# Where the row sums of a pair of heads are finished in a fused attention and expert kernel

## The chip, the cores and the metric

The kernel runs on one core of one Trainium2 chip. The metric is the device time of one execution in microseconds (us); less is better. The engines are TensorE (PE; its weight loads are listed apart as PEld), VectorE (DVE), ScalarE (ACT), GpSimd (POOL) and SyncE (SP, which issues most DMAs). Each engine carries out its own instructions in the order in which the built program holds them and waits at semaphores for the others.

## The reference

Two stages follow each other. The first is causal attention over 8 batches, 8 heads, 576 positions and 64 columns, with a bias from a running sum; the second sends each of the 4608 rows to one of 8 experts.

```python
scores = scale * q @ k.T                       # 576 x 576 for each batch and head
cum = np.cumsum(np.maximum(s, 0.0), axis=-1)
bias = -(cum[:, :, :, None] - cum[:, :, None, :])
scores = np.where(causal, -1000000000.0, scores + np.minimum(bias, 0.0))
attn = np.exp(scores - scores.max(-1))
attn = attn / (np.sum(attn, axis=-1, keepdims=True) + 1e-09)
x = attn @ v                                   # then 4608 x 512
...
h = np.maximum(x[mask] @ w1[e], 0.0)           # for each expert e
out[mask] = gate_w[mask, None] * (h @ w2[e])
```

The division by the row sum plus 1e-9 is the step that is moved here.

## The kernel before, in words

Attention works on 32 pairs. A pair is the same head of two batches, a and b. It is cut into nine chunks: chunk i below 8 holds 128 queries, of batch a for 0 to 3 and b for 4 to 7, against the 128, 256, 384 or 512 keys that the mask leaves; chunk 8, the joint chunk, holds the last 64 queries of both against all 576 keys. The chunks come in the order 3, 7, 2, 6, 8, 1, 5, 0, 4.

For each chunk PE makes the scores in a PSUM tile `sp`, a first product at L376 and a second at L398 (L416 and L417 for the joint chunk, twice two of each). DVE adds the mask and takes the row maximum in one instruction (L400, L422), with a short second one that reads out the maximum. ACT takes the exponent (L431) and leaves the row sum in one column of `sums`; the reading of that sum shows as a second short instruction on ACT.

Three chunks later (`LAG`) PE transposes the exponents into a PSUM tile `pt` (L451; L466 for the joint chunk), of which there are two, used in turn. ACT copies `pt` to `PT` in SBUF (L455); for the joint chunk DVE does (L469, L471). A transpose that wants a `pt` tile therefore waits until the copy from two tiles before is done. Chunks 1 and 5 share one tile and one copy, and so do 0 and 4.

The generator `whole` finishes a pair while the next pair's scores run. One step after the last transposes it makes the value products of PE (L538: into `o` for the first 512 queries of each head, into a tile of the `sp` kind for the last 64), copies `o` by ACT and the other by DVE into `oT`, and yields. At its next step, one chunk later in the text, it takes the row sums: ACT adds `eps`, which holds 1e-9, to the nine columns of `sums` and writes `rs`; DVE takes the reciprocal in place. Then PE multiplies `oT` by a matrix that also holds the router's weights (L350, into `xo`, named `ox` in the profile), and DVE multiplies the result by `rs` into `x` (L560, L562). The second half of the rows (g = 1) goes first, the first half six chunks later (`XLAG`).

What stands where in an engine's queue is decided by a scheduler in the framework, which starts from the order of the code. `issue_after` binds an instruction behind another: the row sums come behind the newest row maximum (`hold`) and the newest exponent (`act`).

Beside this, POOL splits q and k into high and low parts (L326, L330), and the router's steps for a group of eight pairs run in small pieces on DVE, ACT and PE. The experts follow, with matmuls at L1225 and L1199.

Of the kernel before, what the change touches and what calls it, by code (L numbers as in the profile page):

```python
# [7 lines left out]
F32 = mybir.dt.float32  # L8
# [3 lines left out]
AF = mybir.ActivationFunctionType  # L12
# [5 lines left out]
P = 128  # L18
# [24 lines left out]
class Attn:  # L43
# [475 lines left out]
    def whole(self, st):  # L519

        nc = self.nc
        V, PT, x, h = st["V"], st["PT"], st["x"], st["h"]
        for _ in range(TD):
            yield
        o, ox = st["o"], self.ps1.tile([P, 512], F32, name="sp", bufs=SPB)
        oT = self.oT

        pe, self.pe = self.pe, []
        for j in range(5):
            for q0, q1, t, b in ((P * j, 512, o, 0), (512, KW, ox, 512)):  # L530
                if q0 == q1:
                    continue
                for ab in range(2):
                    r = slice(64 * ab, 64 * ab + 64)
                    with ExitStack() as after:
                        for i in pe:
                            after.enter_context(self.tc.issue_after(i))
                        m = nc.tensor.matmul(t[r, q0 - b:q1 - b], V[:, ab, j, :], PT[:, ab, PTS * j + q0 if j < 4 else PTW - 64:PTS * j + q1 if j < 4 else PTW], start=j == 0, stop=j == (4 if b else 3))  # L538
                pe = [m.ins]
        self.wall = m.ins  # L540
        nc.scalar.copy(oT[:, :512], o)
        for ab in range(2):
            r = slice(64 * ab, 64 * ab + 64)
            nc.vector.tensor_copy(oT[r, 512 + 64 * ab:576 + 64 * ab], ox[r, :64])
        yield
        rs = self.sm.tile([P, 9], F32, name="rs")
        with self.tc.issue_after(self.hold[0]), self.tc.issue_after(self.act):
            nc.scalar.activation(rs, st["sums"], AF.Identity, bias=self.eps[:, :1])  # L548
            nc.vector.reciprocal(rs, rs)
        xo = self.xo  # L550
        for g in (1, 0):
            for u in range(2):
                c = 2 * g + u
                with self.tc.issue_after(self.pe[-1]):
                    self.pw_(xo[:, 2 * XW * u:2 * XW * u + 2 * XW], oT[:, P * c:P * c + P], self.pw[:, h, :], start=True, stop=True)
            if g:
                self.pw_(xo[:, 4 * XW:5 * XW], oT[:, 512:], self.pq[:, h, :], start=True, stop=True)
            src = xo[:, :4 * XW].rearrange("p (t d) -> p t d", t=4)
            rv = rs[:, 4 * g:4 * g + 4].unsqueeze(2).broadcast_to([P, 4, XW])
            nc.vector.tensor_tensor(x[g][:, :, :, h], src.rearrange("p t (d r) -> p t d r", r=2), rv.rearrange("p t (d r) -> p t d r", r=2), ALU.mult)  # L560
            if g:
                nc.vector.tensor_scalar(x[2][:, 0, :, h], xo[:, 4 * XW:5 * XW].rearrange("p (d r) -> p d r", r=2), rs[:, 8:9], None, ALU.mult)  # L562
                for _ in range(XLAG if st["pi"] % 8 < 7 and st["pi"] < 30 else 1):
                    yield
# [999 lines left out]
```

## Time and profile before

| what | value |
|---|---|
| median of 3 runs | 785.98 us (785.61 to 785.99) |
| the profiled execution | 786.53 us |
| its span, first to last instruction | 784.8 us |
| PE busy | 772.5 us (98% of the span) |
| PEld busy | 667.4 us (85%) |
| DVE busy | 544.5 us (69%) |
| ACT busy | 501.0 us (64%) |
| POOL busy | 366.3 us (47%) |
| granted TensorE clock, mean | 0.996 |

The profile is of one execution. In its rows, a time in square brackets is how long the engine stood idle before the instruction, and behind the arrow is what ended that. A row of the waits gives the total in us, how often, and the longest. In a timeline the columns are start, duration, engine, line, operation, tiles and shapes, and a count where equal instructions that follow each other are merged. Matmuls overlap, and their ends are modelled, so a row of PE tells when a matmul starts better than when it ends.

### The profile page before, as it was taken

How to read it: one execution, taken by the hardware profiler on the slowest of the kernel's cores; microseconds unless marked ns; L12 is line 12 of the kernel's file. 1: busy time of each engine (PE TensorE's matmuls, PEld its weight loads, DVE VectorE, ACT ScalarE, POOL GpSimd, SP SyncE). 2: the span in 40 equal slices, each digit the busy share in tenths (PEclk: the TensorE clock that was granted, in tenths of full speed). 3: DMA queues.
4: the chain of work that ended last, by engine and by line, in shares of the span. 5: the costliest groups of instructions: out<-in, count | busy, mean ns of one | idle time of the engine just before them, and what ended most of it. 6: DMA issues, size and time to landing. Idle time of an engine off the chain costs nothing. (4 is left out here: it accounts for less than half of the span.)

```text
span 784.8 us, 17146 instructions
## 1 busy us (share of the span) xinstructions
PE 772.5 (98%) x5764; PEld 667.4 (85%) x5764; DVE 544.5 (69%) x1422; ACT 501.0 (64%) x1145; POOL 366.3 (47%) x386
## 2 busy tenths in 40 slices
PE   7999999999999999999999999999999999999997
PEld 6888888888888888888888999998889998998882
DVE  7675577655776667767879797877777877778311
ACT  6877878778787788886565435555555555455211
POOL 8978887898789978994710111110110111110011
PEclk9999999999999999999999999999999999999999
DMA  7477556677567665758979989787788787887760
GB/s 232 133 227 234 189 191 192 212 249 211 163 191 236 211 201 159 248 179 240 324 254 299 325 250 328 249 264 250 238 261 274 250 253 244 271 261 241 256 214 31
DMA packets 88169, 181.21 MB, mean 231 GB/s; under 512 B 13786, under 2 KB 33114, under 8 KB 87951
## 3 DMA queue, kind: packets, MB, share of 16 engines
q1 hardware_dynamic: 82238, 160.03, 65.0%
q0 software_dynamic: 5840, 20.06, 6.6%
q8 instruction: 46, 0.75, 0.4%
q14 instruction: 45, 0.36, 0.1%
HBM read 143.59 MB, written 26.80 MB: 217 GB/s over the span
## 5 line engine op out<-in xcount | busy, mean ns | idle before, releaser
L1211 POOL DMA_INDIRECT out<-ys,oi x36 | 41.1, 1142 | 337.2 <-ACT ys L1210 244.1
L431 ACT ACTIVATE pe<-pe,mx 128x512 f32<-128x512 f32 (+3 forms) x256 | 142.3, 559 | 12.3 <-DVE mx L400 12.2
L400 DVE CUSTOM_DVE_ANT_0 pe<-sp,mk 128x512 f32<-128x512 f32 (+3 forms) x256 | 116.6, 480 | 43.0 <-ACT rs L548 24.0
L455 ACT COPY PT<-pt 128x512 f32<-128x512 f32 (+1 forms) x192 | 94.1, 504 | 26.9 <-PE pt L451 26.9
L451 PE MATMUL pt<-ident,pe 128*128 128x128 f32 x640 | 106.1, 278 | 0.2 <-ACT pe L431 0.2
L376 PE MATMUL sp<-KA,QH 128*128 128x256 f32 (+2 forms) x256 | 98.6, 390 | 1.3 <-POOL KA L240 1.3
L1227 ACT ACTIVATE hT<-hp 128x512 fp32r<-128x512 f32 x72 | 43.1, 599 | 85.9 <-PE hp L1225 85.9
L330 POOL TENSOR_TENSOR QL<-rawq,QH 64x576 fp32r<-64x576 f32 x62 | 87.1, 1422 | 0.3
L330 POOL TENSOR_TENSOR KA<-rawk,KA 64x576 fp32r<-64x576 f32 x62 | 86.4, 1412 | 0.1
L1225 PE MATMUL hp<-xT,wcb 128*128 128x256 f32 x648 | 86.0, 277 | 0.0
L398 PE MATMUL sp<-KB,QL 76*128 76x256 f32 (+2 forms) x256 | 84.1, 330 | 1.7 <-DMA QL<-ek 1.6
L538 PE MATMUL o<-PT,V 128*64 128x512 f32 (+1 forms) x496 | 84.5, 440 | 0.0
L451 PEld LDWEIGHTS pt<-ident,pe 128*128 128x128 f32 x640 | 77.4, 144 | 7.6 <-ACT pe L431 1.4
L1228 DVE SCALAR_TENSOR_TENSOR hT<-hp,hT 128x512 fp32r<-128x512 f32 x72 | 49.5, 688 | 47.1 <-ACT hT L1227 46.7
L1225 PEld LDWEIGHTS hp<-xT,wcb 128*128 128x128 f32 x648 | 79.9, 188 | 0.6
L1199 PE MATMUL y<-wcb,hT 128*128 128x512 f32 x336 | 79.5, 393 | 0.0
L1199 PEld LDWEIGHTS y<-wcb,hT 128*128 128x128 f32 x336 | 62.5, 188 | 13.2
L1225 PE MATMUL hp<-xT,wca 128*128 128x256 f32 x528 | 72.3, 277 | 0.0
L1225 PEld LDWEIGHTS hp<-xT,wca 128*128 128x128 f32 x528 | 66.0, 188 | 0.7 <-DVE hT L1228 0.2
L538 PEld LDWEIGHTS sp<-PT,V 128*64 128x64 f32 x620 | 38.2, 137 | 33.3 <-issue 28.8
L1225 PE MATMUL hp<-xT,wcc 128*128 128x256 f32 x456 | 63.0, 277 | 1.5 <-DVE hT L1228 1.5
L1199 PE MATMUL y<-wca,hT 128*128 128x512 f32 x264 | 62.3, 392 | 0.0
(294 smaller groups left out, 1633.8 us busy)
## 6 DMA issues: line engine op xcount, KB each, us to landing
wrbw<-in_w SPq DMA_DIRECT2D x94, 512.0 KB
wraw<-in_w SPq DMA_DIRECT2D x50, 512.0 KB
rawq<-in_qkv SPq DMA_DIRECT2D x31, 576.0 KB
rawk<-in_qkv SPq DMA_DIRECT2D x31, 576.0 KB
V<-in_qkv SPq DMA_DIRECT2D x32, 320.0 KB
KB<-KA SPq DMA_DIRECT2D x62, 144.0 KB
xr<-lists SPq DMA_DIRECT2D x68, 128.0 KB
wcb<-in_w SPq DMA_DIRECT2D x10, 512.0 KB
```

Of the source, the lines that this page charges most:

```text
L330: self.last = nc.gpsimd.tensor_tensor(o, i, h, ALU.subtract).ins
L376: self.pe.append(self.nc.tensor.matmul(sp[:, :nn], QH[:, q0:q0 + P], self.KA[u][:, ab, :nn], start=True, stop=False).ins)
L398: self.pe.append(nc.tensor.matmul(sp[:, :nn], QL[:EXT, q0:q0 + P], KB[:EXT, ab, :nn], start=False, stop=True).ins)
L400: ins = nc.vector.tensor_tensor_reduce(out=t[:, :n], in0=sp[:, :n], in1=self.mk[:, 512 - n:512], scale=-0.125, scalar=3.0e38, op0=ALU.add, ...
L431: self.act = nc.scalar.activation(t[:, :n], t[:, :n], AF.Exp, bias=m, scale=-1.0, accum_out=st["sums"][:, o:o + 1]).ins
L451: self.pe.append(nc.tensor.transpose(out=pt[:, o:o + P], in_=pe[:, P * j:P * j + P], identity=self.ident).ins)
L455: return cp(w[:, :, :, v:v + P], pt[:, :n * (1 + both)].rearrange("p (a j q) -> p a j q", a=1 + both, q=P))
L538: m = nc.tensor.matmul(t[r, q0 - b:q1 - b], V[:, ab, j, :], PT[:, ab, PTS * j + q0 if j < 4 else PTW - 64:PTS * j + q1 if j < 4 else PTW], ...
L1199: self.last[0] = nc.tensor.matmul(y[u], hT[:, a, f, P * u:P * u + P], W[4 + f // 2][:, c, 512 * (f % 2):512 * (f % 2) + 512], start=f == 0 ...
L1225: nc.tensor.matmul(hp[:, u], W[k][:, a, f:f + P], xT[:, c, k], start=k == 0 and i == 0, stop=k == 3 and i == 2)
L1227: hi = nc.scalar.activation(hs, hp, AF.Relu)
L1228: lo = nc.vector.scalar_tensor_tensor(hT[:, 1, 2 * m:2 * m + 2], hp, 0.0, hs.bitcast(F32), ALU.max, ALU.subtract)
```

## The change

Four lines of `whole` move up: the row sums and their reciprocal are written into the program ahead of the copies of the value products instead of behind the yield that follows them. The same instructions are issued with the same shapes.

```diff
         self.wall = m.ins
+        rs = self.sm.tile([P, 9], F32, name="rs")
+        with self.tc.issue_after(self.hold[0]), self.tc.issue_after(self.act):
+            nc.scalar.activation(rs, st["sums"], AF.Identity, bias=self.eps[:, :1])
+            nc.vector.reciprocal(rs, rs)
         nc.scalar.copy(oT[:, :512], o)
         for ab in range(2):
             r = slice(64 * ab, 64 * ab + 64)
             nc.vector.tensor_copy(oT[r, 512 + 64 * ab:576 + 64 * ab], ox[r, :64])
         yield
-        rs = self.sm.tile([P, 9], F32, name="rs")
-        with self.tc.issue_after(self.hold[0]), self.tc.issue_after(self.act):
-            nc.scalar.activation(rs, st["sums"], AF.Identity, bias=self.eps[:, :1])
-            nc.vector.reciprocal(rs, rs)
         xo = self.xo
```

In the changed kernel the row sums are line 543, the reciprocal 544, the ACT copy 545 and the DVE copies 548. The scheduler gives another order than the text alone would tell. On ACT, at the end of a pair (here the twenty-first; the `pe` tile is that of the next pair's chunk 1, numbered 3807 before and 3810 in the change):

```order
-L541 COPY oT<-o 128x512
-L455 COPY PT_110<-pt 128x4x128
-L431 ACTIVATE pe_3807,sums<-pe_3807,mx 128x256
-L548 ACTIVATE rs<-sums,eps 128x9
+L543 ACTIVATE rs<-sums,eps 128x9
+L545 COPY oT<-o 128x512
+L455 COPY PT_110<-pt 128x4x128
+L431 ACTIVATE pe_3810,sums<-pe_3810,mx 128x256
 L455 COPY PT_110<-pt 128x3x128 x2
```

The row sums stood between the exponent of chunk 1 and the two copies of chunks 2 and 6; now they stand ahead of the copy of the value products, and those two copies follow the exponent. A few rows further on ACT (`pe_3827`, `pe_3839` and `pe_3854` are chunks 5, 0 and 4 of the same next pair, `pe_3862` is chunk 3 of the pair after that):

```order
 L431 ACTIVATE pe_3827,sums<-pe_3827,mx 128x256
 L431 ACTIVATE pe_3839,sums<-pe_3839,mx 128x128
-L455 COPY PT_110<-pt 128x2x2x128
 L431 ACTIVATE pe_3854,sums<-pe_3854,mx 128x128
+L455 COPY PT_110<-pt 128x2x2x128
 L431 ACTIVATE pe_3862,sums<-pe_3862,mx 128x512
```

The copy of chunks 1 and 5 has moved behind the exponent of chunk 4. On PE, a little later (`pe_3862` again, and the joint chunk of its pair):

```order
 L376 MATMUL sp<-KA_105,QH_101 128x384
 L398 MATMUL sp<-KB_107,QL_103 128x384
-L416 MATMUL sp<-KA_105,QH_101 128x288
-L417 MATMUL sp<-KB_107,QL_103 128x288
 L451 MATMUL pt<-ident,pe_3862 128x128 x4
+L416 MATMUL sp<-KA_105,QH_101 128x288
+L417 MATMUL sp<-KB_107,QL_103 128x288
 L416 MATMUL sp<-KA_105,QH_101 128x288
 L417 MATMUL sp<-KB_107,QL_103 128x288
```

The four transposes of chunk 3 have moved ahead of the first two matmuls of the joint chunk. This piece of the difference is found in 19 pairs. In six others, those in which router work falls, more rows move: the two transposes of chunks 0 and 4 follow each other where matmuls stood between them. On DVE the reciprocal stands ahead of the copies of the value products, and L560 and L562 of the half g = 1 stand behind the first L400 that follows those copies instead of behind the third. The DMA queue of SP differs in three places, where neighbouring issues change places, POOL not at all, and the expert stage on no engine.

## The prediction

> **What bounds the kernel now.** I read the page first, then busy times by stage, then the waits, then one pair of heads in order of time. By stage (columns: the stretch in us, its length, busy time and count of PE, PEld, DVE, ACT, POOL, then granted clock, DMA share, GB/s):
>
> ```profile
> 26.00:353.00 327.00, 326.98 (x2864) 274.29 (x2865) 219.66 (x927) 264.36 (x800) 279.15 (x294) 1.00 0.65 203
> 385.00:760.00 375.00, 373.54 (x2452) 339.24 (x2451) 276.90 (x369) 195.20 (x250) 43.53 (x38) 1.00 0.82 267
> ```
>
> The first row is the attention stage, where the change lies; the second is nearly all of the expert stage. PE is busy 326.98 of 327.00 us, so whatever delays PE in attention lengthens the span, and what only moves time on DVE or ACT costs nothing. But the ends of matmuls are modelled in this profile, so a short delay can hide inside a "busy" PE. The row of weight loads (PEld) does not hide it. The waits, all engines together (us in total, times, longest):
>
> ```profile
> PEld pt L466 <- ACT PT L455: 5.0, 30, 0.2
> DVE pe L400 <- ACT rs L548: 24.0, 26, 0.9
> PEld pt L451 <- ACT pe L431: 1.4, 5, 0.4
> ```
>
> The largest DVE row, 24.0 us behind the row sums on ACT (L548), looks like the target. It is idle time of an engine that is not the bound. The row to watch is the first: 30 times, once in nearly every pair, the transposes of the joint chunk (L466) wait for an ACT copy (L455), 5.0 us in all. One pair in order of time:
>
> ```profile
> 248.59 0.49 PE L451 MATMUL pt<-ident,pe 128*128 128x128 f32 x3
> 248.65 0.51 ACT L431 ACTIVATE pe<-pe,mx 128x256 f32<-128x256 f32 x1 [0.19 <-DVE mx L400]
> ...
> 249.07 0.18 ACT L431 ACTIVATION_READ_ACCUMULATOR pe<-pe,mx 128x1 f32 x1
> ...
> 249.16 0.29 ACT L548 ACTIVATE rs<-sums,eps 128x9 f32<-128x9 f32 x1
> ...
> 249.35 0.83 ACT L455 COPY PT<-pt 128x384 f32<-128x384 f32 x2
> ...
> 249.48 0.42 DVE L400 CUSTOM_DVE_ANT_0 pe<-sp,mk 128x256 f32<-128x256 f32 x1 [0.93 <-ACT rs L548]
> ...
> 249.62 0.28 PE L398 MATMUL sp<-KB,QL 76*128 76x256 f32 x1
> ...
> 249.86 0.42 PEld L466 LDWEIGHTS pt<-ident,pep 128*128 128x128 f32 x4 [0.16 <-ACT PT L455]
> 249.86 0.66 PE L466 MATMUL pt<-ident,pep 128*128 128x128 f32 x4
> ...
> 250.36 0.27 PE L466 MATMUL o<-ident,pep 128*64 128x128 f32 x1
> ```
>
> ACT does the row sums (249.16) between an exp and the two copies. The first copy frees the PSUM tile that L466 needs, and PE, done with its scores at L398, stands before L466. One pair is its own counter-example, because there ACT did that first copy ahead of the exp:
>
> ```profile
> 325.80 0.28 PE L398 MATMUL sp<-KB,QL 76*128 76x256 f32 x1
> 325.82 0.47 PEld L466 LDWEIGHTS pt<-ident,pep 128*128 128x128 f32 x4
> ...
> 325.93 0.60 PE L466 MATMUL pt<-ident,pep 128*128 128x128 f32 x4
> ...
> 326.36 0.27 PE L466 MATMUL o<-ident,pep 128*64 128x128 f32 x1
> ```
>
> From L398 to the fifth transpose PE takes 250.36 - 249.62 = 0.74 us with the wait and 326.36 - 325.80 = 0.56 us without: the wait costs PE 0.18 us in a pair, 30 x 0.18 = 5.4 us in all.
>
> **The change part by part.** No instruction is added or removed. Per pair, one ACT instruction and one DVE instruction go forward, and other rows move around them. Their prices:
>
> ```profile
> L548 ACT ACTIVATE rs<-sums,eps x31: 287/287/291, 31.6 to 357.6; 128x9 f32<-128x9 f32 x31
> L549 DVE RECIPROCAL rs<-rs x31: 208/210/213, 32.2 to 358.3; 128x9 f32<-128x9 f32 x31
> ```
>
> *The row sums leave their place between exp and copies (ACT).* The next copy starts 249.35 - 249.16 = 0.19 us after the row sums start, so their slot is 0.19 us, less than their 287 ns. The copies move up by 0.19. Their transposes are no hindrance: the first copy's end at 248.59 + 0.49 = 249.08. The weight load of L466 now stands at 249.86; unhindered it follows L398 by 0.02, as at 325.80 and 325.82, thus at 249.64. That is 0.22 of lateness, of which 0.19 goes: 0.03 may stay, 30 x 0.03 = 0.9 us. So this part gives 5.4 - 0.9 = 4.5 us, with ends of 5.4 (nothing stays) and, with twice the residue, 3.6.
>
> The Trainium skill, "TensorE: Matmul & The Clock Gate", section "Architectural detail: the array is 16× 32×32, not 1× 128×128", says that a matmul can begin before its weight load completes. By that rule only the late start of the first transpose would count, 249.86 - 249.62 = 0.24 us after L398 against 325.93 - 325.80 = 0.13, or 0.11 x 30 = 3.3 us instead of 5.4. The start of the fifth transpose speaks against that: 0.18 is lost there, so the late load is paid as well.
>
> *The row sums arrive ahead of the copy of the value products (ACT, DVE).* The place they go to, in one of the pairs that is tightest on ACT:
>
> ```profile
> 202.87 0.19 ACT L431 ACTIVATION_READ_ACCUMULATOR pep<-pep,mx 128x1 f32 x1
> ...
> 203.70 0.59 ACT L541 COPY oT<-o 128x512 f32<-128x512 f32 x1 [0.64 <-PE o L538]
> ...
> 203.88 0.46 DVE L544 COPY oT<-sp 64x64 f32<-64x64 f32 x2 [0.48 <-PE sp L538]
> ```
>
> The sums start at about 202.97, end at 203.26, before the 203.70 at which PE lets the copy go; the reciprocal then takes 203.29 to 203.50, before 203.88. Both are hidden by the value products. What waits behind the reciprocal on DVE is the pair of copies L544, and behind these the projection on PE:
>
> ```profile
> 214.85 0.30 DVE L792 TENSOR_TENSOR_SCAN ahead<-go,ohb 128x80 bf16<-128x80 bf16 x1
> 215.17 0.23 DVE L544 COPY oT<-sp 64x64 f32<-64x64 f32 x1
> ...
> 215.70 0.31 PEld L350 LDWEIGHTS ox<-pq,oT 128*128 128x128 f32 x2
> ```
>
> Here DVE is full with routing work, and 0.21 more could push the last copy from 215.40 to 215.61; L350 with pq needs it at 215.70. The cover holds by 0.09 us; if it did not, the price is at most 0.21 in each of the three pairs that route inside the loop, 0.6 us. I take nothing.
>
> *The multiplies by the reciprocal move up on DVE (L560, L562).* They fall into the idle 0.93 us before 249.48. This brings the later chunks forward, and it matters for the next part.
>
> *The order of PE and ACT changes.* In 19 of the pairs the four transposes of the next pair's first chunk now stand directly behind L398, ahead of two 288-column matmuls (L416, L417); on ACT the exp of the last 128-wide chunk now stands ahead of a copy. The rows that decide whether PE meets a new wait there:
>
> ```profile
> 250.73 0.68 DVE L469 COPY PT<-pt 128x512 f32<-128x512 f32 x1
> ...
> 251.18 0.60 PE L451 MATMUL pt<-ident,pe 128*128 128x128 f32 x4
> ...
> 251.52 0.27 DVE L400 CUSTOM_DVE_ANT_0 pe<-sp,mk 128x128 f32<-128x128 f32 x1
> ...
> 251.82 0.59 ACT L455 COPY PT<-pt 128x512 f32<-128x512 f32 x1 [0.75 <-PE pt L451]
> ...
> 252.30 0.40 ACT L431 ACTIVATE pe<-pe,mx 128x128 f32<-128x128 f32 x1
> ...
> 252.70 0.71 ACT L431 ACTIVATE pe<-pe,mx 128x512 f32<-128x512 f32 x1
> ...
> 253.31 0.19 ACT L431 ACTIVATION_READ_ACCUMULATOR pe<-pe,mx 128x1 f32 x1
> 253.33 0.34 PE L398 MATMUL sp<-KB,QL 76*128 76x384 f32 x1
> 253.34 0.19 PEld L416 LDWEIGHTS sp<-KA,QH 128*128 128x128 f32 x1
> ...
> 253.51 0.30 PE L416 MATMUL sp<-KA,QH 128*128 128x288 f32 x1
> ...
> 253.66 0.50 PEld L451 LDWEIGHTS pt<-ident,pe 128*128 128x128 f32 x4
> ```
>
> Today the transposes load at 253.66, after their exp (252.70) is complete at 253.50. In their new place they would load at 253.34, or 253.19 with PE ahead by 4.5/30 = 0.15. How early the exp gets there: with DVE relieved, L469 starts when its transposes end (249.86 + 0.66 - 0.15 = 250.37, and 0.04 to be seen), at 250.41 instead of 250.73, so the reduction at 251.52 moves to 251.20 and its maximum is there at 251.49. ACT is idle then (0.75 before 251.82), so the small exp starts at 251.52 instead of 252.30, the copy 0.40 later at 251.92 (its transposes end at 251.78 - 0.15), and the wide exp 0.48 later at 252.40: 0.30 earlier, complete at 253.20. How soon PE follows an exp:
>
> ```profile
> 198.69 0.19 ACT L431 ACTIVATION_READ_ACCUMULATOR pe<-pe,mx 128x1 f32 x1
> ...
> 198.93 0.14 PEld L451 LDWEIGHTS pt<-ident,pe 128*128 128x128 f32 x1 [0.21 <-ACT pe L431]
> ```
>
> 0.05 us after its end, so the load is at 253.25 instead of 253.19, 0.06 late. The 384-column matmul ahead of it covers that: L416 loads at 253.34 but its matmul starts only at 253.51, 0.17 later, where a load by itself takes 0.11 (325.82 to 325.93), so 0.06 is free. Cover and lateness are equal within the rows' reading; I take 0.02 as left, 19 x 0.02 = 0.4 us. The ends are nothing and, if the 0.06 counts whole and as much again, 19 x 0.12 = 2.3 us.
>
> On SP three issues change places with a neighbour; the moved step has no DMA of its own, and PE's row of waits above is for ACT, so I take nothing for it.
>
> *The sum.* 5.4 - 0.9 - 0.4 = 4.1 us less. The profiled execution took 786.53 us (span 784.8 and 1.7 around it), 0.55 above the median of 785.98; the saving is of its attention stage and is carried over unchanged: 785.98 - 4.1 = 781.9. The forecast's own ends: 785.98 - 5.4 - 0.6 = 780.0, where the other 0.6 are the waits of 0.21 as at 198.93 in three pairs whose split transposes the new order joins; and 3.6 - 2.3 = 1.3 saved, 784.7.
>
> **The rivals.**
>
> *The wait moves to the transposes that were brought forward (slower).* If the small exp does not get ahead of its copy in time, because the reduction at 251.52 keeps its time, the wide exp stays at 252.70, and PE stands at 253.19 until 253.55: 0.36, less 0.06 of cover, 0.30 in each of 19 pairs, 5.7 us, against 4.5 gained: 785.98 + 1.2 = 787.2. It decides from 4.5/19 = 0.24 us a pair. For it speaks that 1.4 us of exactly this wait is there today; against it that DVE has 0.93 idle just ahead and ACT 0.75. Chance 0.08.
>
> *PE's gain is given back (no change).* A shorter attention stage could only bring the next limit forward: POOL, 279.15 of 327 us busy, or the transfers of expert weights, at a share of 0.82. Time 786.0. Against it: POOL's 279.15 us would fit into a stage 15% shorter, and 4.1 of 327 us is 1.3%; and in the expert stage PE is busy 373.54 of 375 us, so it would be paced by itself from an earlier start. Chance 0.12.
>
> *Only the late start counts.* If the loss per wait is 0.11, the gain is 3.3 - 0.9 - 0.4 = 2.0 us, 784.0, still faster. Chance 0.10. This is the mechanism of the page named above; the fifth transpose speaks against it.
>
> *The change does nothing, as the row of 24.0 us is DVE idle time.* True of that row, but ACT's slot moves too; this is in the second rival's chance.
>
> **How the numbers follow.** Forecast 0.70, at 781.9. About 0.2%, 1.6 us, is what a measurement of this kernel can tell from no change, so faster means under 784.4. Forecast and late-start rival are faster: 0.80. The second rival is the same: 0.12. The first is slower: 0.08. The range goes from 780.0, where nothing stays of the waits, to 785.2, above the forecast's own high end of 784.7; it leaves out the slower and the unchanged case, 0.20 in all.
>
> **What would show it.** Right: the row of L466 waiting for L455 falls from 5.0 us to under 1; DVE's 24.0 us behind the row sums is gone; a pair takes about 0.15 us less from one value product to the next. Wrong: transposes L451 waiting for the exp L431 for far more than 1.4 us, some 19 times; or L466 still waiting about 0.16 each time, which would mean that the copy was not held by the row sums; or an attention stage that is shorter and an end that is not.

## The result, and the profile after

The changed kernel takes 781.64 us, the median of 7 runs (780.89 to 783.70), against 785.98 us for 7 runs of the kernel before (785.26 to 787.29). The ratio is 0.9949 (95% interval 0.9939 to 0.9958), a gain of 0.42 to 0.61%. The forecast was 781.9. The profiled execution is the median run itself, 781.64 us with a span of 779.9.

The waits of the changed kernel, all engines (us in total, times, longest):

```profile
DVE rs L544 <- ACT rs L543: 24.4, 21, 1.5
...
PEld pt L451 <- ACT pe L431: 0.9, 2, 0.4
...
PEld o L466 <- ACT pep L431: 0.2, 1, 0.2
```

The row that carried the forecast, L466 waiting for L455 30 times, is gone. So is DVE's row of 24.0 us; in its place DVE stands 24.4 us before the reciprocal. Neither of these two rows of DVE has to do with the gain (below, e10 and e11). The stages (stretch, length, busy time and count of PE, PEld, DVE, ACT, POOL, then clock, DMA share, GB/s):

```profile
26.00:350.00 324.00, 323.95 (x2894) 274.06 (x2892) 232.78 (x931) 269.68 (x805) 281.36 (x295) 1.00 0.67 206
385.00:756.00 371.00, 369.30 (x2423) 335.22 (x2422) 273.00 (x365) 192.63 (x247) 40.07 (x35) 1.00 0.81 265
```

PE is still the bound, just as full; it gets through more matmuls in the same time (2894 records in 324 us, against 2842 in the same stretch before). One pair in order of time, with the DVE row that ends the reduction of chunk 1 in front:

```profile
244.16 0.08 DVE L400 DVE_READ_ACCUMULATOR2_ANT mx<- 128x1 f32 x1
...
244.28 0.51 ACT L431 ACTIVATE pe<-pe,mx 128x256 f32<-128x256 f32 x1
...
244.70 0.19 ACT L431 ACTIVATION_READ_ACCUMULATOR pe<-pe,mx 128x1 f32 x1
...
244.81 1.05 ACT L455 COPY PT<-pt 128x384 f32<-128x384 f32 x2
...
245.30 0.28 PE L398 MATMUL sp<-KB,QL 76*128 76x256 f32 x1
245.34 0.44 PEld L466 LDWEIGHTS pt<-ident,pep 128*128 128x128 f32 x4
...
245.42 0.60 PE L466 MATMUL pt<-ident,pep 128*128 128x128 f32 x4
...
245.85 0.27 PE L466 MATMUL o<-ident,pep 128*64 128x128 f32 x1
```

ACT goes from the exponent straight to the two copies. L466 loads 0.04 behind L398 and waits for nothing; from L398 to the fifth transpose PE takes 0.55 us, as in the one pair of the kernel before that had no wait (0.56).

Two numbers are read from every trace below. The pair: from the first value product (L538) of a pair to that of the next, median of 14 pairs without router work. The stretch: from L398 to the fifth L466 behind it, median of the same pairs.

| kernel | time, us | ratio to before (95%) | pair, ns | stretch, ns |
|---|---|---|---|---|
| before | 785.98 | 1 | 10833 | 735 |
| changed | 781.64 | 0.9949 (0.9939 to 0.9958) | 10639 | 562 |
| e1, reciprocal late | 783.07 | 0.9962 (0.9948 to 0.9975) | 10664 | 592 |
| e3, slot filled | 784.63 | 0.9982 (0.9971 to 0.9992) | 10746 | 683 |
| e5, multiplies late | 784.34 | 0.9982 (0.9970 to 0.9994) | 10726 | 560 |
| e10, no second wait | 785.20 | 0.9984 (0.9973 to 0.9995) | 10760 | 675 |
| e9, no addition | 783.84 | 0.9965 (0.9952 to 0.9977) | 10692 | 600 |
| e11, neither of the two | 781.47 | 0.9936 (0.9922 to 0.9950) | 10655 | 560 |
| e2, addition on DVE | 798.63 | 1.0155 (1.0141 to 1.0168) | 10693 | 603 |
| e2b, the same, immediate | 799.40 | 1.0164 (1.0148 to 1.0179) | 10688 | 600 |
| e7a, router's addition early | 781.37 | 0.9930 (0.9919 to 0.9942) | 10640 | 561 |

Each ratio is to runs of the kernel before on the same chip (medians there 786.23, 786.12 and 786.33). Over the 30 intervals between pairs the two profiled executions differ by 326.07 - 320.99 = 5.08 us, their spans by 4.9. Of the 5.08, 0.4 is in the third to the sixth pair, which took 0.1 longer than the other pairs before and do not now.

### The profile page after: what moved, and what is told of

It reads as the page before. It is cut to its first block, busy times and chain, and to the rows that moved or that the text cites. A ratio compares the mean times of both kernels' runs of the same rounds, so it can differ in the third digit from the quotient of the medians.

```text
span 779.9 us, 17053 instructions
## 1 busy us (share of the span) xinstructions
PE 765.9 (98%) x5764; PEld 664.3 (85%) x5764; DVE 554.9 (71%) x1422; ACT 505.0 (65%) x1145; POOL 366.8 (47%) x386
## 5 line engine op out<-in xcount | busy, mean ns | idle before, releaser
L400 DVE CUSTOM_DVE_ANT_0 pe<-sp,mk 128x512 f32<-128x512 f32 (+3 forms) x256 | 119.2, 485 | 18.6 <-PE sp L398 10.9
L455 ACT COPY PT<-pt 128x512 f32<-128x512 f32 (+1 forms) x192 | 97.0, 506 | 12.5 <-PE pt L451 9.8
L451 PE MATMUL pt<-ident,pe 128*128 128x128 f32 x640 | 103.8, 276 | 0.8 <-ACT PT L455 0.5
L538 PE MATMUL o<-PT,V 128*64 128x512 f32 (+1 forms) x496 | 84.5, 440 | 0.0
L451 PEld LDWEIGHTS pt<-ident,pe 128*128 128x128 f32 x640 | 75.5, 143 | 10.0 <-ACT PT L455 0.9
L398 PE MATMUL sp<-KB,QL 76*128 76x256 f32 (+2 forms) x256 | 83.5, 328 | 0.0
L538 PEld LDWEIGHTS sp<-PT,V 128*64 128x64 f32 x620 | 38.2, 137 | 33.3 <-issue 28.8
L1199 PE MATMUL y<-wcc,hT 128*128 128x512 f32 x264 | 62.2, 391 | 0.0
```

Of the source, the lines that this page charges most:

```text
L398: self.pe.append(nc.tensor.matmul(sp[:, :nn], QL[:EXT, q0:q0 + P], KB[:EXT, ab, :nn], start=False, stop=True).ins)
L400: ins = nc.vector.tensor_tensor_reduce(out=t[:, :n], in0=sp[:, :n], in1=self.mk[:, 512 - n:512], scale=-0.125, scalar=3.0e38, op0=ALU.add, ...
L451: self.pe.append(nc.tensor.transpose(out=pt[:, o:o + P], in_=pe[:, P * j:P * j + P], identity=self.ident).ins)
L455: return cp(w[:, :, :, v:v + P], pt[:, :n * (1 + both)].rearrange("p (a j q) -> p a j q", a=1 + both, q=P))
L1199: self.last[0] = nc.tensor.matmul(y[u], hT[:, a, f, P * u:P * u + P], W[4 + f // 2][:, c, 512 * (f % 2):512 * (f % 2) + 512], start=f == 0 ...
```

## The experiments

The theory (T) is the forecast's: the row sums held ACT for 0.19 us between the exponent of chunk 1 and the copies, and L466 on PE paid for it. The rival (R) is what the largest row of the reductions' waits suggests: DVE stood 0.9 us behind the row sums in 26 pairs, and the earlier sums let it run ahead.

**The slot filled again (e3).** The changed kernel with one more instruction of the same shape where the row sums used to be:

```diff
+        r2 = self.sm.tile([P, 9], F32, name="r2")
+        with self.tc.issue_after(self.hold[0]), self.tc.issue_after(self.act):
+            nc.scalar.activation(r2, st["sums"], AF.Identity, bias=self.eps[:, :1])
         xo = self.xo
```

> The changed kernel plus one more ACT instruction of the row sums' shape (128x9, into a tile that nobody reads) in the place that the row sums left, between exp and copies. Rows of DVE and PE stand as in the changed kernel. T: the slot of 0.19 us is back, the 30 waits of L466 for L455 are back at about 0.16 each, 785.5 to 786.5. R: DVE keeps its early sums, so the gain stays, 781.6 to 782.4.

Measured: 784.63 us, between the two theories. R is out as the whole story, since sums and multiplies on DVE are as early as in the changed kernel and most of the gain is gone. But T is not whole either: pairs are 107 ns longer than in the changed kernel, and still 87 ns shorter than before. One pair of e3 in order of time:

```profile
247.70 0.08 DVE L400 DVE_READ_ACCUMULATOR2_ANT mx<- 128x1 f32 x1
...
247.82 0.51 ACT L431 ACTIVATE pe<-pe,mx 128x256 f32<-128x256 f32 x1
...
248.33 0.29 ACT L552 ACTIVATE r<-sums,eps 128x9 f32<-128x9 f32 x1
...
248.52 0.88 ACT L455 COPY PT<-pt 128x384 f32<-128x384 f32 x2
...
248.84 0.28 PE L398 MATMUL sp<-KB,QL 76*128 76x256 f32 x1
...
249.03 0.42 PEld L466 LDWEIGHTS pt<-ident,pep 128*128 128x128 f32 x4
```

The slot is back (248.33 to 248.52, 0.19), and L466 loads 0.19 behind L398. Before it was 0.24. Something else had moved the copy 0.05 earlier. It is in the first two rows: the exponent starts 0.12 after the read-out of the maximum, in the kernel before (248.47 and 248.65 in the next lines) it started 0.18 after. From the start of the reduction to that of the exponent it is 527 to 530 ns in 29 pairs before, and 466 to 470 in every pair but the first of the changed kernel and of e3. One pair of the kernel before:

```profile
248.47 0.08 DVE L400 DVE_READ_ACCUMULATOR2_ANT mx<- 128x1 f32 x1
...
248.65 0.51 ACT L431 ACTIVATE pe<-pe,mx 128x256 f32<-128x256 f32 x1 [0.19 <-DVE mx L400]
```

The cause shows in the list of all instructions of the exponents' line, which also has those of ACT's queue that only wait. Before (the second line is that of the reductions on DVE, for later):

```profile
L431 ACTq EVENT_SEMAPHORE  x150: 17/17/17, 34.8 to 357.1; - x150
L400 DVEq EVENT_SEMAPHORE  x34: 21/21/21, 15.2 to 357.9; - x34
```

and in the changed kernel:

```profile
L431 ACTq EVENT_SEMAPHORE  x120: 17/17/17, 34.0 to 346.4; - x120
L400 DVEq EVENT_SEMAPHORE  x5: 21/21/21, 15.2 to 24.4; - x5
```

Thirty fewer on ACT, one for each of 30 pairs. In the trace of those pairs the wait-only instruction waits for DVE, that is for the maximum, and the exponent of chunk 1 behind it for ACT itself. The second wait is for ACT's exponent of a pair ago that last used its buffer (e10, below, bears this out). That had ended some 10 us earlier, so the wait was met, but it had to be passed: in 29 of the 30 pairs the exponent starts 62 or 63 ns after the start of its wait-only instruction. In the changed kernel it carries the wait for DVE alone; the row sums, which wait for a later exponent, now stand ahead and cover the other. The Trainium skill, "Perfetto Trace Analysis", section "Identifying Dependency Chains", says that instructions which wait on several engines may get such instructions put ahead of them; the trace agrees, and it gives the price, 0.06 us from maximum to exponent. That is theory T2: the slot and the second wait.

**The second wait taken away, the slot left (e10).** The kernel before, with a third buffer for the tile of chunks 1 and 5, so that the exponent that used it last is older and already covered; `rs` gives up a buffer to make room. The order of the rows on PE, ACT, DVE and POOL is that of the kernel before.

```diff
-            t = self.wk.tile([P, n], F32, name=f"pe{c}")
+            t = self.wk.tile([P, n], F32, name=f"pe{c}", **({"bufs": 3} if c == 1 else {}))
...
-        rs = self.sm.tile([P, 9], F32, name="rs")
+        rs = self.sm.tile([P, 9], F32, name="rs", bufs=2)
```

> The kernel before, with a third buffer for the 256-wide score tiles (and two instead of three for rs, to make room). Every engine's instructions stand in the old order, the row sums stay in their old slot; what goes is only a wait-only instruction, on ACT ahead of the exp of chunk 1 in 30 pairs (the traces before had that exp 528 to 530 ns after its reduction starts, the changed kernel 467 to 470), and one on DVE ahead of the second 256-wide reduction. Theory T (the slot alone): no change, 786. Theory T2 (slot plus second wait): the exp follows its reduction by 469 instead of 529 ns, L466 comes 0.05 earlier behind L398 (240 to about 190 ns), 0.05 to 0.09 less in each of 30 pairs, 783.5 to 784.7. R (DVE's 0.9-us wait is what cost): that wait goes, most of the gain comes, 782 to 783.

Measured: 785.20 us, above T2's 783.5 to 784.7; the ratio of 0.9984 makes it 784.7 against the 785.98 of before, 0.4 to 2.1 us less by its interval. The pairs say what T2 said: 73 ns shorter (2.2 us in 30), 182 ns from L398 to L466 instead of 240, the exponent 466 to 470 ns after its reduction, in all pairs but two. Its profiled run was its slowest, 787.35, with 1.7 us lost ahead of the first pair. The wait-only instructions of e10, and then the waits of DVE for its reductions:

```profile
L431 ACTq EVENT_SEMAPHORE  x120: 17/17/17, 36.6 to 352.2; - x120
L400 DVEq EVENT_SEMAPHORE  x6: 21/21/21, 17.5 to 33.5; - x6
```

```profile
DVE pe L400 <- PE sp L398: 35.9, 55, 5.9
...
DVE pe L400 <- PE pt L451: 5.7, 7, 0.8
...
DVE pe L400 <- ACT rs L548: 0.9, 1, 0.9
```

One pair of e10:

```profile
249.77 0.29 ACT L548 ACTIVATE rs<-sums,eps 128x9 f32<-128x9 f32 x1
...
249.96 0.89 ACT L455 COPY PT<-pt 128x384 f32<-128x384 f32 x2
250.04 0.42 DVE L400 CUSTOM_DVE_ANT_0 pe<-sp,mk 128x256 f32<-128x256 f32 x1 [0.81 <-PE pt L451]
...
250.29 0.28 PE L398 MATMUL sp<-KB,QL 76*128 76x256 f32 x1
...
250.47 0.42 PEld L466 LDWEIGHTS pt<-ident,pep 128*128 128x128 f32 x4
```

R falls here for good, and the name of its row turns out to be wrong. The row sums stand where they stood and DVE's wait for them is gone (0.9 us left of 24.0): the reduction of chunk 5 starts at 250.04, before the row sums end at 250.06. In the kernel before it has a wait-only instruction ahead, 28 of the 34 on DVE listed above. That one waits for PE, that is for the scores, and the reduction behind it for ACT; the reduction starts 105 or 106 ns after it every time, and two of the 28 times it starts before the row sums end. So DVE stood there for the scores and then passed a second wait. The profile put the whole idle time down to the row sums, since they ended last before it. In e10 nearly the same idle time (0.81 here, 0.93 before) is put down to PE, most of it in the row of the scores: 35.9 us, 18.4 before. The reduction of chunk 5 starts 5.07 us into the pair instead of 5.18. e10 takes the second waits of both engines away, so the 73 ns are for both; the stretch from L398 to the fifth transpose alone is 60 ns shorter.

The list of waits also has a hole. L466 loads 0.18 behind L398, 0.14 later than in the changed kernel (0.04), and no bracket tells of it; e10 has no row of L466 waiting for L455, nor has e3. Waits of 0.16 were listed and these are not, so that row at zero is no proof that nothing is waited for. The distance between the two starts is.

**The slot emptied (e9), and both costs taken away (e11).** e9 leaves out the addition on ACT and keeps the reciprocal in its old place in the text. e11 is e9 with the buffers of e10.

```diff
-            nc.scalar.activation(rs, st["sums"], AF.Identity, bias=self.eps[:, :1])
-            nc.vector.reciprocal(rs, rs)
+            nc.vector.reciprocal(rs, st["sums"])
```

> The kernel before without the addition of 1e-9 to the row sums of a pair (that part of the computation is left out); the reciprocal reads the sums directly, in its old place on DVE two chunks later. ACT's slot between exp and copies is empty, and DVE has no instruction more. T and T2: the gain of the changed kernel without moving anything forward, L466 without its wait, less what a second wait ahead of the first 256-wide reduction costs (0.11 on DVE, 0.03 a pair in the run with the late reciprocal): 782 to 783.5. R: sums and multiplies are as late as before on DVE, no gain, 785.5 to 786.5.

> The kernel before with both suspected costs taken away and nothing moved: no addition of 1e-9 (that part is left out, so ACT's slot is empty) and the third buffer for the 256-wide score tiles (no wait-only instruction ahead of the exp of chunk 1, none ahead of the first 256-wide reduction). T2 (slot and second waits are the whole of it): pairs of 10640 to 10660 ns as in the changed kernel, 782.0 within 1, clearly below the run without the addition alone (pairs of about 10690, 783.84). If something else that the forward move brings is needed (early sums, moved transposes), pairs stay at 10680 or more and the time at 783.5 or more.

Measured: e9 783.84 us with pairs of 10692, e11 781.47 with pairs of 10655. So the gain of the change comes without early row sums, by taking the two costs away.

It does not come without another order, though nothing is moved in the text: in both runs the scheduler orders PE as in the changed kernel, but for one transpose, and ACT too, but for the row sums, so the transposes of chunk 3 are brought forward here as well. On DVE the reciprocal stands between the reductions of chunks 1 and 5. The two runs in which nothing else moves are e3, in the order of the changed kernel, and e10, in that of the kernel before. From the changed kernel to e3 the slot is worth 10746 - 10639 = 107 ns a pair; from the kernel before to e10 the second waits are worth 10833 - 10760 = 73. Together 180 of the 194 ns that the change gave; what the other 14 are is not shown. The new order by itself is worth next to nothing by these runs: from e10 to e11 it and the slot together give 10760 - 10655 = 105 ns, against the 107 of the slot alone.

e9 falls short of e11. What differs in the first part of a pair is a second wait on DVE ahead of the first of the two reductions, which starts 0.11 later (3.93 us into the pair instead of 3.82).

**The reciprocal back in its old place in the text (e1).** On DVE it stands there behind the reduction of chunk 1, in the kernel before behind that of chunk 5; PE is ordered as in the changed kernel but for one transpose.

```diff
             nc.scalar.activation(rs, st["sums"], AF.Identity, bias=self.eps[:, :1])
-            nc.vector.reciprocal(rs, rs)
...
         yield
+        with self.tc.issue_after(self.hold[0]), self.tc.issue_after(self.act):
+            nc.vector.reciprocal(rs, rs)
```

> Of the changed kernel only the row sums on ACT keep their early place; the reciprocal goes back to its old place on DVE, and with it the multiplies start later again. Theory T (the gain is the 0.19-us ACT slot between the exp of chunk 1 and the L455 copies, which L466's transposes on PE waited for): the whole gain stays, 781.6 within 0.8, and the wait of L466 for L455 stays at 0. Rival R (the gain comes from DVE, which no longer waits 0.9 us in 26 pairs and so has maxima and multiplies earlier): the reciprocal is held behind the first reduction again, most of the gain goes, 784 to 786.

Measured: 783.07 us, where T said 781.6 within 0.8 and R 784 to 786. Pairs are 25 ns longer than in the changed kernel. The reciprocal's place does matter, but in the way of e9:

```profile
L400 DVEq EVENT_SEMAPHORE  x30: 21/21/21, 14.6 to 352.1; - x30
```

30 wait-only instructions ahead of reductions, 5 in the changed kernel; 25 of the 30 are ahead of chunk 1's, which starts 0.11 later, the exponent and the copies with it, and the stretch is 592 instead of 562 ns.

**The multiplies late (e5).** The changed kernel, with L560 and L562 of the half g = 1 held behind the next reduction. The transposes of chunk 3 stay brought forward; on ACT the exponent of chunk 4 stands behind a copy again, as before the change.

```diff
+            if g:
+                yield
...
-            nc.vector.tensor_tensor(x[g][:, :, :, h], ...)
+            with self.tc.issue_after(self.hold[0]):
+                nc.vector.tensor_tensor(x[g][:, :, :, h], ...)
...
-                for _ in range(XLAG if st["pi"] % 8 < 7 and st["pi"] < 30 else 1):
+                for _ in range(XLAG - 1 if st["pi"] % 8 < 7 and st["pi"] < 30 else 1):
```

> The changed kernel with the multiplies of value products by the reciprocals put behind the next chunk's reduction on DVE, so that the reductions go first and the multiplies no longer use the DVE time that the early reciprocal freed; the transposes that the change brought forward on PE stay brought forward in 19 pairs. T: no change, 781.0 to 782.5, since DVE's order is off PE's path as long as the transposes' exp is in time; the exp of the 128-wide chunk stands behind a copy on ACT again, and if that makes the exp of the moved transposes late, a wait of L451 for L431 of up to 0.3 in 19 pairs appears, up to 5.7 us, 787. R: the gain needs early multiplies and is lost, 785 to 786.

Measured: 784.34 us, pairs 87 ns longer than in the changed kernel, the stretch unchanged at 560. The loss is where the forecast's first rival put it:

```profile
PEld pt L451 <- ACT pe L431: 4.9, 23, 0.4
```

```profile
250.91 0.19 ACT L431 ACTIVATION_READ_ACCUMULATOR pe<-pe,mx 128x1 f32 x1
250.94 0.34 PE L398 MATMUL sp<-KB,QL 76*128 76x384 f32 x1
...
251.15 0.42 PEld L451 LDWEIGHTS pt<-ident,pe 128*128 128x128 f32 x4 [0.20 <-ACT pe L431]
```

The wide exponent is complete at 251.10, and the transposes that were brought forward stand 0.20 before it. In the changed kernel at the same place:

```profile
248.67 0.19 ACT L431 ACTIVATION_READ_ACCUMULATOR pe<-pe,mx 128x1 f32 x1
...
248.83 0.34 PE L398 MATMUL sp<-KB,QL 76*128 76x384 f32 x1
...
248.91 0.47 PEld L451 LDWEIGHTS pt<-ident,pe 128*128 128x128 f32 x4
249.01 0.60 PE L451 MATMUL pt<-ident,pe 128*128 128x128 f32 x4
```

The exponent is complete at 248.86, and the load at 248.91 stands 0.05 behind it, as in e5. It does so in all 19 pairs, after 0.06 to 0.07 of idle time on PEld, too short for the list of waits. But the first transpose starts 0.18 behind L398, as L416 did in that place before (253.33 and 253.51 in the prediction's rows), so this wait is covered. In e5 it starts about 0.21 behind in most pairs. What the early multiplies are good for is this: they let the small exponent get ahead of its copy, and so the wide one.

**The addition on DVE (e2, e2b).** The kernel before, with the addition in its old place but on DVE. e2 adds the tile `eps`, e2b an immediate:

```diff
-            nc.scalar.activation(rs, st["sums"], AF.Identity, bias=self.eps[:, :1])
+            nc.vector.tensor_tensor(rs, st["sums"], self.eps, ALU.add)            # e2
+            nc.vector.tensor_scalar(rs, st["sums"], 1.0e-9, None, ALU.add)        # e2b
```

> The kernel before, with the addition of 1e-9 to the row sums still two chunks of scores later, but on DVE instead of ACT: the ACT slot between exp and copies is empty, and DVE has two small instructions in the old place instead of one. T: as fast as the changed kernel, 781.6 within 1, with no wait of L466 for L455. R: no gain, since DVE gets its sums no earlier and has about 0.2 us more work in each of 31 pairs, 786 to 788.

> As the kernel before with the addition of 1e-9 on DVE in its old place, but as a tensor_scalar with the number as an immediate, so with one operand from SBUF instead of two. In the run with two operands the 128x9 addition took 164 to 6874 ns, each long one ending 29 to 38 ns after a tensor_tensor or tensor_scalar on POOL. If two SBUF operands make DVE wait for POOL, every addition takes under 250 ns here and the time is that of the kernel with the early row sums and late reciprocal, 782.5 to 784. The Trainium skill, SBUF — State Buffer, section Who interferes with whom, lists tensor_scalar too among those that can take the pair of ports shared with POOL, by its two-port mode; by that rule some of the 31 additions wait up to several us again and the time is 790 to 799.

Measured: 798.63 and 799.40 us, slower than before by 1.4 to 1.8%, and by neither theory: L466 lost its wait (stretch 603 and 600), pairs are 10693 and 10688. The loss lies in a few pairs, above all the last three. All 31 additions of e2, and the worst with what POOL did then:

```profile
L548 DVE TENSOR_TENSOR rs<-sums,eps x31: 164/182/6874, 30.9 to 366.6; 128x9 f32<-128x9 f32 x31
```

```profile
347.09 6.87 DVE L548 TENSOR_TENSOR rs<-sums,eps 128x9 f32<-128x9 f32 x1
...
347.26 2.06 POOL L1077 TENSOR_SCALAR wca<-wraw 128x1024 fp32r<-128x1024 f32 x2
...
349.30 4.63 POOL L1080 TENSOR_TENSOR wca<-wraw,wca 128x1024 fp32r<-128x1024 f32 x2
...
354.00 0.22 DVE L549 RECIPROCAL rs<-rs 128x9 f32<-128x9 f32 x1
```

An addition of nine columns took 6.87 us: it ended with four instructions of POOL that follow each other without a gap, at 353.96 against 353.93. Of the 31, seven took over 0.6 us, and each ended 24 to 37 ns after an instruction of POOL. Above the median of 0.182 they add up to 13.6 us; e2 is 14.8 slower than e9, which has no addition. e2b, with one operand in SBUF instead of two, does the same at the same place:

```profile
347.74 6.87 DVE L548 TENSOR_SCALAR rs<-sums 128x9 f32<-128x9 f32 x1
...
347.90 2.06 POOL L1077 TENSOR_SCALAR wca<-wraw 128x1024 fp32r<-128x1024 f32 x2
...
349.93 4.63 POOL L1080 TENSOR_TENSOR wca<-wraw,wca 128x1024 fp32r<-128x1024 f32 x2
```

So it is not the second operand. The Trainium skill, "SBUF — State Buffer", section "Who interferes with whom", says that DVE and GpSimd share a pair of ports as a lock that is held for a whole instruction, and names both forms among those that can take it; both runs agree. The reciprocal of the same tile took at most 217 ns in these runs. This is what the addition on ACT spares, and for e2 both T and R were beside the point.

**The router's addition moved too (e7a).** What the freed slot showed: in the three pairs that route, another 128x9 addition of ACT (L795) now stands in it. The changed kernel:

```profile
212.49 0.29 ACT L795 ACTIVATE gs<-gs,eps 128x9 f32<-128x9 f32 x1
...
212.68 0.89 ACT L455 COPY PT<-pt 128x384 f32<-128x384 f32 x2
...
213.01 0.28 PE L398 MATMUL sp<-KB,QL 76*128 76x256 f32 x1
...
213.19 0.42 PEld L466 LDWEIGHTS pt<-ident,pep 128*128 128x128 f32 x4
```

These pairs take 11012 to 11020 ns; before the change they took 10926. e7a brings L795 one step forward:

```diff
-        for _ in range(2 if mm else 0):
+        for _ in range(1 if mm else 0):
             yield False
         nc.scalar.activation(gs, gs, AF.Identity, bias=self.eps)
-        for _ in range(2 if mm else 0):
+        for _ in range(3 if mm else 0):
             yield False
```

> The changed kernel with one instruction more moved: in the three pairs that route (9, 17, 25) the router's own 128x9 addition on ACT (L795) goes from the freed slot to a place behind the early row sums, ahead of the copy of the value products. Order on PE, DVE, POOL and SP is unchanged. T and T2: the three pairs lose the wait that came back there (L466 184 ns behind L398 instead of 120, 11012 to 11020 ns from pair to pair), 0.1 to 0.2 less in each, 0.3 to 0.6 us in all, 781.2; if the router's sum on DVE comes too late for the new place, the copy behind it is late and these pairs get longer by up to 0.3 each, 782.5.

Measured: 781.37 us, ratio 0.9930. The three pairs take 10906 to 10913 ns, and L466 is free:

```profile
213.34 1.06 ACT L455 COPY PT<-pt 128x384 f32<-128x384 f32 x2
...
213.84 0.29 PE L398 MATMUL sp<-KB,QL 76*128 76x256 f32 x1
213.87 0.46 PEld L466 LDWEIGHTS pt<-ident,pep 128*128 128x128 f32 x4
```

3 x 0.11 = 0.3 us is shown in the pairs. That the whole kernel is faster than the changed one by as much can't be told by its time: the intervals, 0.9919 to 0.9942 and 0.9939 to 0.9958, overlap.

**The changed kernel again (a2).**

> The changed kernel as it is, once more, for comparison on the same chip: 781.6 within 0.7, pairs of 10620 to 10650 ns.

Measured: 782.86 us, ratio 0.9953 (0.9938 to 0.9968), somewhat above what was expected, with pairs of 10640 ns. In its profiled run the fourth and the fifth pair took 0.9 us more than in the first one; several runs have such a spot between the third and the sixth pair. Its cause is open.

## Why the prediction was right, point by point

- *PE is the bound, and the row of L466 is the one to watch, not DVE's 24.0 us.* Right. e10 took DVE's wait away and left L466 most of its delay, and most of the time stayed. But the 24.0 us were read by their name: DVE stood there for the scores and passed a second wait, and did not wait for the row sums (e10). Nor is it DVE's largest row; the copies L544 waited 49.8 us for the value products.
- *5.4 us gross, 0.18 a pair.* Right in size: the stretch fell from 735 to 562 ns, 0.173 a pair. But the step's cause was only one of two. The slot is worth 0.107 a pair (e3), the second waits 0.073 (e10). The forecast put the whole 0.18 down to the slot, which by itself gives 30 x 0.107 = 3.2 us.
- *0.9 us stays, since the slot of 0.19 is shorter than the lateness of 0.22.* Wrong. Nothing stays. The step looked only at the instruction that left; the exponent ahead of it came 0.06 earlier as well, as it lost its wait-only instruction, and 0.19 + 0.06 is more than 0.22. e3 shows the arithmetic from the other side: with the slot back, 0.05 of the lateness is still gone.
- *0.4 us for the transposes brought forward in 19 pairs.* Not paid. Cover and lateness came out as equal as the rows had it: in the 19 pairs the load waits 0.06 to 0.07 for its exponent, and the matmul ahead covers all of it. e5 shows that the rival was real: where the small exponent keeps its place behind the copy, the same transposes wait 4.9 us in 23 cases, and a pair costs 87 ns more. It stayed below its break-even of 0.24 a pair even then.
- *Reciprocal ahead of the copies: nothing.* Right. What the forecast missed in the three routing pairs is on ACT: L795 dropped into the freed slot, and they became 0.09 longer, 0.3 us in all. One more pair, the 28th, became 0.17 longer: in its new order PE stands idle for 0.25 ahead of the projection L350, which needs the copy of the value products.
- *Only the late start counts (rival, 784.0).* Refuted by e3: L466 starts 65 ns later than in the changed kernel (189 against 124), and the fifth transpose 121 ns. The late load is paid besides, so the rule that the forecast weighed (the Trainium skill, "TensorE: Matmul & The Clock Gate", section "Architectural detail: the array is 16× 32×32, not 1× 128×128") does not price this wait.
- *The gain is given back (rival).* No. 30 intervals give 5.08 us, the span 4.9.
- *A pair takes about 0.15 us less.* It is 0.194. The sum of 4.1 took off 1.3 us that was not lost (0.9 and 0.4) and missed 0.5 us that was; 4.3 was measured by the medians, and the ratios of the two runs, 0.9949 and 0.9953, make it 4.0 and 3.7. That the forecast came out within 0.3 us is in part luck: the slot by itself gives 3.2 us, and the second waits, a cost that it did not see, went away with it and made up for that.

## What to carry to other kernels

A short instruction costs where it stands: 0.19 us on an engine that is 64% busy was worth about 3 us, because PE waited behind it in 30 pairs. The row of 24.0 us on DVE was for the most part time in which the scores were not there yet, under the name of an instruction that merely ended last; where a row names one of several waits, take it away and see what is listed in its place. Where an instruction moves, look also at which waits move with it: a second wait that is met long ago still is an instruction ahead of the one that matters, and an earlier instruction on the same engine that waits for something later removes it. And look at what falls into the freed place.

## What the runs showed of the hardware

- A second wait costs time although it is long met. With a wait-only instruction ahead, the exponent on ACT starts 0.06 us later after its reduction (528 ns instead of 468). On DVE a reduction starts 105 or 106 ns after the start of its wait-only instruction, in all 28 pairs of the kernel before that have one (chunk 5) and in all 25 of e1 and of e9 (chunk 1), and 0.11 later in the pair than without one.
- A weight load that is held back costs more than the lateness of its matmul: 65 ns late at the first transpose became 121 at the fifth (e3).
- An addition of 128x9 on DVE waits for POOL's whole instructions, up to 6.87 us, with a tile or with an immediate as its second operand; the reciprocal of the same tile did not (at most 217 ns).
- The list of waits leaves out short ones: in e3 and e10 loads that came 0.14 to 0.15 late have no row, while 0.16 had one. And it can name the wrong instruction: the 24.0 us of DVE behind the row sums.
